# Attention and a spectral gate on one core: three batches' DMA transposes moved from SyncE's queue to ScalarE's, with a new hand-tuned order

## The chip, the cores and the metric

The kernel runs on one core of one Trainium2 chip. The metric is the device time of one execution in microseconds, as the median of several runs; smaller is better. The profile is that of a single execution on the same core, so its span (382.9 us) is a little under the median of the runs.

## What is computed

Eight batches of an attention with 12 heads (448 rows, 64 columns a head) feed a gated spectral filter:

```python
scores = q @ k.T / 8;  m = max(scores);  e = exp(scores - m)
x = (e / (sum(e) + exp(-m))) @ v          # per head, then heads side by side: 448 x 768
x1, x2, x3 = split(x @ w_proj, 3)          # 768 -> 3 * 768
x2 = irfft(rfft(x2) * rfft(filter))        # a circular convolution over the 448 rows
out = (x1 * x2 * x3) @ w_out               # 448 x 768, float32
```

All matmuls are in bf16. The softmax runs without the maximum: numerator and denominator are multiplied by exp(m), so the denominator is sum(e) + 1.

## The kernel before, in words

**The work.** Heads go in pairs, six pairs to a batch, 48 in all. For one pair TensorE forms the scores with the keys on partitions (L773, and L775 for the keys left over, which both heads share), ScalarE takes their exponentials into bf16 (L780, L786), TensorE multiplies them with v (L798 for the shared keys, L806 for the rest), and VectorE divides by the sum (L819 to L821) and writes the tile `xb`, rows on partitions. The dense part wants x with its columns on partitions, in the tile `xT`. There are two ways from `xb` to `xT` (`attention`, end): four TensorE transposes into PSUM (L901) and a copy back (L908 on ScalarE, L910 on VectorE), or one DMA transpose of two or three pairs (`x_dma`, L892). Which of them is taken is set by `XALL`: a batch in it turns all six pairs by DMA; another batch from the third on turns five by DMA and the last on TensorE; the first two turn all on TensorE.

**The dense part of a batch** is in `dense(b)`: VectorE folds `xT` (L950 to L958), TensorE forms x2 from the folded columns (L981, or L1011 and a DMA transpose back, L1028, in the last four batches), ScalarE and VectorE carry the spectrum (L1049, L1057, L1063, L1069), TensorE forms the gates x1 and x3 (`gate`, L1095), ScalarE copies x1 out (L1107), VectorE multiplies by x3 (L1110); TensorE goes back from the spectrum (L1134, L1143), VectorE unfolds and multiplies into `yT` and `yR` (L1152 to L1178), and TensorE multiplies with w_out (L1207). ScalarE copies that to `osb` (L1219), and SyncE stores it (L1226; L1229 for the 64 rows left over, which two batches share). The dense part of a batch runs between the attention of later batches.

**Loads and other transposes.** From the third batch on q, k and v come as DMA loads (q on GpSimd's queue, L536; k and v on SyncE's, L585, then cast to bf16 on GpSimd, L590 and L602), and q and k are turned by DMA transposes on SyncE's queue (L542, four to a batch; L547, two blocks of 12 x 128 columns to a batch from the fourth on). All DMA transposes of the kernel before stand in SyncE's queue.

**What sets the order.** Nothing is scheduled by loops. Every piece of work is a task with an engine, a cost, a wanted time and the tokens that it needs and makes (`add`). `Plan.run` plays the tasks through at the written costs, lets each engine take the first of its tasks, in the order of wanted times, whose needs are met, and hands out PSUM banks. The tasks of each engine are emitted in that order, and each engine then works its own list strictly from the top. The wanted times come from the tables at the head of the kernel (`ATT`, `SLOT`, `DENSE`, `PACE`, `FOLD`, `LEAD`, ...), `late` is an extra landing time that the planner books for a transfer. The waits between engines are put in by the framework when the program is built. In the gaps that the planner sees in the first 36 us it puts small matmuls on a tile of zeros (L1332).

**The end.** In the last batch the rows 256 to 383 (block 2) come last. `O_last` writes them in three pieces, of 384, 192 and 192 columns, copies the last piece on VectorE and stores each by itself.

Of the kernel before, what the change touches and what calls it, by code (L numbers as in the profile page):

```python
# [19 lines left out]
D = H * DH  # L20
SP = 112
NST = S // SP
NDT = D // 128
NHP = H // 2
SCALE = 1.0 / float(np.sqrt(DH))
DCH = 384
# [15 lines left out]
class Plan:  # L42
# [26 lines left out]
    def add(self, eng, cost, want, emit, need=(), make=(), take=(), give=(), dma=0.0, run=256, n=1, after=0.0, begun=(), late=0.0):  # L69
        self.tasks.append((want, len(self.tasks), eng, cost, emit, need, make, take, give, dma, after, run, n, begun, late))  # L70
# [186 lines left out]
def kernel(  # L257
# [11 lines left out]
    nc = tc.nc  # L269
# [1 line left out]
    MAGIC = 12582912.0  # L271
    NSTAGED = 2
    SPIN = 38
    EARLY1 = 2.19
    ATT = [0.75, 24.41, 87.21, 101.61, 150.77, 186.69, 235.26, 286.49]
    SLOT = [2.52, 8.01, 4.27, 4.82, 6.44, 0.30, 6.71, 5.19]
    DENSE = [46.81, 84.00, 123.83, 169.80, 218.58, 253.46, 313.76, 296.92]
    PACE = [2.16, 2.30, 2.04, 2.28, 1.15, 2.55, 0.60, 1.33]
    FOLD = [-0.20, 0.45, -42.13, -39.60, 2.51, 0.15, -6.85, 0.77]
    BPS = 1.67  # L280
    RE1 = 22.20
    WT = 1.31
    FT = 21.96
    HALVED = (2,)
    AHEAD = [0, 0, 33.95, 43.62, 34, 34, 34, 34]
    LEAD = [-14.87, 8.62, 5.03, 10.66]
    LOADS = ((1, 0), (1, 1), ("F", None), (0, None), (2, None), ("O", None))
    LOAD = [22.29, 18.40, 18.46, 37.27, 38.16, 45.94]
    STEP = 2.26
    BYCOL = (4, 5, 6, 7)  # L290
    GLAST = 40.00
    XALL = (3, 4, 5, 6, 7)
    FOLD0 = (52.22, 39.65, 43.44)

    const = ctx.enter_context(tc.tile_pool(name="const", bufs=1))
    wts = ctx.enter_context(tc.tile_pool(name="wts", bufs=1))
# [16 lines left out]
    wout_bf = wts.tile([128, NDT, D], BF16, name="wout_bf")  # L313
# [8 lines left out]
    kT = [const.tile([128, NHP, 4, 128], BF16, name=f"kT{i}") for i in range(2)]  # L322
# [14 lines left out]
    nf = nat.bitcast(F32)  # L337
# [13 lines left out]
    add = plan.add  # L351
# [4 lines left out]
    def bank(hy):  # L356
        i = plan.banks[hy][0]
        return psum[:, 512 * i : 512 * i + 512]
# [167 lines left out]
    def loaded(b):  # L526
# [3 lines left out]
        parts = 2 if b in HALVED else 1  # L530
        size = NHP // parts
        few = 1 if b == NSTAGED else 3
# [20 lines left out]
        n = 0  # L553
# [21 lines left out]
        for hp in range(NHP):  # L575
            g = i0 + hp
            for n, (name, x) in enumerate((("k", k), ("v", v))):
                slot = 2 * (g - NHP * NSTAGED) + n
                at = (KNAT + NST * D) // 2 + 384 * (slot % 5)
                src = nf[:, at : at + 384]  # L580
                old = slot - 5
                room = [("c" + "kv"[old % 2], NHP * NSTAGED + old // 2)] if old >= 0 else [
                    ("c" + w, i) for w in "kqv" for i in range(NHP * NSTAGED - 2, NHP * NSTAGED)]
                add("SP", 0.52, tau(g) - LEAD[0] + 0.1 * n,
                    lambda x=x, hp=hp, src=src: nc.sync.dma_start(src.rearrange("p (u c) -> p u c", u=2), rows(x, b, hp)),  # L585
                    need=room, make=[("s" + name, g)], dma=0.7, run=768)
                sv = src.rearrange("p (u j d) -> p u j d", u=2, j=3)
                if name == "k":
                    add("POOL", 0.6, tau(g) - LEAD[1],
                        lambda hp=hp, sv=sv: nc.gpsimd.tensor_copy(  # L590
                            kn[:, hp, 1:4].rearrange("p j (u d) -> p u j d", u=2), sv
                        ),
                        need=[("sk", g)] + (["zero kn"] if b == NSTAGED else [("kT", g - NHP)]), make=[("ck", g)])
                    if hp % few == 0:
                        gs = range(g, g + few)
                        add("SP", 1.3, tau(g) - LEAD[2], lambda hp=hp: k_turn(hp), need=[("ck", i) for i in gs] + [("crk", b), last],
                            make=[("kT", i) for i in gs], dma=0.6 * few, late=0.7)
                else:

                    def cast(hp=hp, sv=sv):  # L600
                        for u in range(2):
                            nc.gpsimd.tensor_copy(vn[b % 2][:, hp, 4 * u : 4 * u + 3, 0:DH], sv[:, u])  # L602

                    add("POOL", 0.72, tau(g) - LEAD[3], cast, need=[("sv", g), ("V", g - 2 * NHP, 1)], make=[("cv", g), ("v", g)])
# [104 lines left out]
    W = {}  # L709
# [51 lines left out]
    def attention(i):  # L761
# [127 lines left out]
        def x_dma():  # L889
            x, xb = xT(), W["xb", b]  # L890
            gs = slice(0 if hp < 3 else 3, hp + 1)
            nc.sync.dma_start(  # L892
                x[:, gs, :].rearrange("p g (t n) -> p (g t) n", t=NST),
                xb[:, gs].rearrange("p g t c -> p (g t c)"),
                transpose=True,
            )
# [18 lines left out]
        if b in XALL or b > 1 and hp < NHP - 1:  # L915
            if hp in (2, NHP - 1 if b in XALL else NHP - 2):
                ps = range(0, 3) if hp == 2 else range(3, hp + 1)
                add("SP", 1.3, w, x_dma, need=[("xb", NHP * b + h) for h in ps] + old,
                    make=[m for h in ps for m in (("X", NHP * b + h), ("xT", b, h))], dma=0.5 * len(ps), late=1.2)
        else:  # L920
            add("PE", 0.23, w, x_pe, need=[("xb", i)], make=[("X", i)], take=[("hy", ("X", i))])
            add("ACT" if on_act else "DVE", 0.43 if on_act else 0.33, w - 1.0, x_back, need=[("X", i)] + old, make=[("xT", b, hp)], give=[("hy", ("X", i))])


    def dense(b):

        L = {}
        at = [0.0, 0]

        def span(cost):  # L930

            w = DENSE[b] + at[0] * PACE[b]
            at[0] += cost
            return w
# [9 lines left out]
        def hold(key):  # L944
            return ("hy", key)
# [88 lines left out]
        def PT(dt):  # L1034
            hy = hold(("PT", b, dt))
            w = span(1.15)
            add("PE", 1.15, w, lambda: columns(dt, hy), need=[("xf", b, pg) for pg in range(4)] + [("w", 1, ch) for ch in range(2)],
                make=[("PT", b, dt)], take=[hy], give=[("xf", b)])
            add(("ACT", "DVE")[dt % 2], (0.43, 0.55)[dt % 2], w, lambda: columns_back(dt), need=[("PT", b, dt)],
                make=[("x2T", b, dt // 3)], give=[hy])  # L1040
            if dt % 3 == 2:
                ch = dt // 3
                add("SP", 1.3, w, lambda: rows_back(ch), need=[("x2T", b, ch)], make=[("x2", b, pg, ch) for pg in range(4)],
                    take=[("x2", b)], dma=1.5, late=1.2)

        def spectrum(pg, ch, hy):
            K = BLK_K[pg]
# [199 lines left out]
            if ch == 1:  # L1247
                add("SP", 0.6, w, lambda: store(st), need=[("os", b, st)], make=[("store", b, st)], give=[os_], dma=1.4, run=3072)

        def O_last(st):  # L1250
            rs = slice(st * 128, (st + 1) * 128)
            parts = ((0, DCH, "ACT"), (DCH, DCH // 2, "ACT"), (DCH + DCH // 2, DCH // 2, "DVE"))
            for n, (at, size, by) in enumerate(parts):
                hy = hold(("O", b, st, n))
                w = span(0.97 * size / DCH)
                c = slice(at, at + size)

                def product(hy=hy, c=c, size=size, n=n):
                    L["O", st, n] = bank(hy)
                    for dt in range(NDT):  # L1260
                        nc.tensor.matmul(
                            L["O", st, n][:, 0:size], W["yT", b][:, dt, rs], wout_bf[:, dt, c], start=(dt == 0), stop=(dt == NDT - 1)
                        )

                def back(size=size, c=c, n=n, by=by):
                    (nc.scalar.copy if by == "ACT" else nc.vector.tensor_copy)(nf[:, c], L["O", st, n][:, 0:size])

                def store_part(c=c, n=n):
                    (nc.scalar if n == 1 else nc.sync).dma_start(out[b, rs, c], nf[:, c])

                add("PE", 0.98 * size / DCH, w, product, need=[("y", b, 0), "wout"], make=[("O", b, st, n)], take=[hy],
                    give=[("yT", b)])
                add(by, (0.38, 0.25, 0.28)[n], w, back, need=[("O", b, st, n)], make=[("os", b, st, n)], give=[hy])
                add("ACT" if n == 1 else "SP", 0.6, w, store_part, need=[("os", b, st, n)], make=[("store", b, st, n)],
                    dma=1.4 * size / D, run=1536)

        if b and b + 1 < n_batches:
            G(0, 0), G(0, 1)
        if b in BYCOL and b + 1 == n_batches:
# [21 lines left out]
        for dt in range(NDT):  # L1301
            I(dt), G(2 + (dt + 1) // 2, (dt + 1) % 2)
        G(5, 1)
        for st in range(3) if b % 2 == 0 and b + 1 < n_batches else (0, 1, 3, 2) if b + 1 == n_batches else range(4):
            if (b, st) == (n_batches - 1, 2):
                O_last(st)
                continue
            for ch in range(2):
                O(st, ch)


    E = mybir.EngineType
# [103 lines left out]
```

## Time and profile before

| | before |
|---|---|
| median of 3 runs | 385.62 us (385.33 to 387.34) |
| span of the profiled execution | 382.9 us |
| TensorE busy | 366.5 us (96%), 3678 matmuls |
| ScalarE busy | 261.2 us (68%) |
| VectorE busy | 258.0 us (67%) |
| GpSimd busy | 112.5 us (29%) |
| DMA moved | 62.53 MB, mean 163 GB/s |

Engines are written PE (TensorE matmuls), PEld (its weight loads), DVE (VectorE), ACT (ScalarE), POOL (GpSimd) and SP (SyncE); SPq and ACTq are the DMA issues of an engine. In a list of waits, "PE psum L1095 <- DMA xT<-xb" says that a matmul of line 1095 sat idle until a transfer from `xb` to `xT` had landed. In a timeline a row has start, length, engine, line, operation and tiles, and in brackets the idle time ahead of it with what ended it. A chain of waits is followed back from the last instruction, at each step to what released it.

### The profile page before, as it was taken

Reading aid. Unit: us, or ns where it says so; the run is one execution under the profiler, and the core shown is the slowest. Engines: PE = TensorE matmul, PEld = TensorE weight load, DVE = VectorE, ACT = ScalarE, POOL = GpSimd, SP = SyncE. Lnnn points to the kernel's source line nnn. Section 1 sums busy time; section 2 is a strip of 40 time slices with the busy share of each in tenths; the row PEclk is TensorE's granted clock in tenths of the full one; section 3 lists DMA queues with packets and bytes.
Section 4 is the critical chain, followed back from the end, with each engine's and each line's share of the span. In section 5 each row is a group of like instructions: output and inputs, shape, how many; then the busy total and the mean of one; then the engine's idle time right before and its main releaser. Section 6 shows DMA issues by size and latency. Waiting matters only on the chain.

```text
span 382.9 us, 9526 instructions
## 1 busy us (share of the span) xinstructions
PE 366.5 (96%) x3678; PEld 225.7 (59%) x3678; DVE 258.0 (67%) x671; ACT 261.2 (68%) x456; POOL 112.5 (29%) x232
## 2 busy tenths in 40 slices
PE   8879999999999999959999999999999999999995
PEld 7557765566655675635675555555555655655553
DVE  6587589945789549747367964783469936982880
ACT  5867875756877878845688846675788758633633
POOL 6695465032464434704345350000000000000000
PEclk9998999999999999998999999999999999999999
DMA  8999999999999999999899998942341034046205
GB/s 214 276 258 249 227 204 210 117 138 247 203 201 220 138 294 235 176 150 276 232 220 159 206 235 140 174 128 84 84 85 34 9 96 113 6 80 137 111 0 166
DMA packets 149965, 62.53 MB, mean 163 GB/s; under 512 B 114525, under 2 KB 146464, under 8 KB 149920
## 3 DMA queue, kind: packets, MB, share of 16 engines
q1 hardware_dynamic: 112352, 52.05, 63.0%
q0 software_dynamic: 37184, 9.54, 25.4%
q8 instruction: 29, 0.48, 0.5%
q10 hardware_dynamic: 384, 0.33, 0.3%
q14 instruction: 16, 0.13, 0.1%
HBM read 43.86 MB, written 11.01 MB: 143 GB/s over the span
## 4 chain that ended last, share of the span: by engine, by line
PE 81%; DVE 8%; DMA 4%; issue 3%; SPq 1%; ACT 1%; POOL 1%; DVEq 0%; POOLq 0%
PE psum L1095 25%; PE psum L1207 13%; PE psum L806 9%; PE psum L981 8%; PE psum L773 7%; PE psum L1011 7%; PE psum L1049 3%; DMA xT<-xb 2%; PE psum L1134 2%; PE psum L775 2%; DMA nat<-in_q_dram 2%; PE psum L798 1%; DVE xb L821 1%; DVE xf L958 1%; PE psum L901 1%
## 5 line engine op out<-in xcount | busy, mean ns | idle before, releaser
L780 ACT ACTIVATE e<-psum 128x896 bf16<-128x896 f32 x144 | 125.6, 925 | 23.1 <-PE psum L773 22.0
L1095 PE MATMUL psum<-xT,wproj_bf 128*128 128x448 bf16 x576 | 121.9, 354 | 5.1 <-DMA xT<-xb 4.2
L1095 PEld LDWEIGHTS <-wproj_bf 128*128 128x128 bf16 x576 | 54.6, 98 | 51.5 <-issue 8.3
L1207 PE MATMUL psum<-wout_bf,yT 128*128 128x384 bf16 x276 | 50.6, 326 | 0.0
L1107 ACT CAST x<-psum 128x448 bf16<-128x448 f32 x48 | 25.8, 537 | 29.8 <-PE psum L1095 27.1
L806 PE MATMUL psum<-vn,e 128*128 128x65 bf16 x1152 | 45.3, 195 | 0.0
L1219 ACT COPY osb<-psum 128x384 f32<-128x384 f32 x54 | 25.2, 483 | 23.9 <-PE psum L1207 23.4
L773 PE MATMUL psum<-qT,kT 64*128 64x448 bf16 x288 | 41.1, 356 | 0.0
L806 PEld LDWEIGHTS <-e 128*128 128x128 bf16 x1152 | 39.5, 98 | 2.6
L1063 DVE TENSOR_TENSOR t<-xs,hrs 113x768 bf16<-113x768 bf16 (+1 forms) x64 | 33.5, 563 | 8.6 <-ACT xs L1057 8.4
L602 POOL CAST vn<-nat 128x192 bf16<-128x192 f32 x72 | 28.2, 418 | 34.8 <-DMA nat<-in_v_dram 25.3
L819 DVE TENSOR_SCALAR rec<-psum 128x8 f32<-128x8 f32 x48 | 7.8, 163 | 44.7 <-PE psum L806 33.8
L1207 PEld LDWEIGHTS <-yT 128*128 128x128 bf16 x276 | 26.2, 97 | 18.2 <-issue 1.1
L536 POOL DMA_DIRECT2D nat<-in_q_dram x28 | 24.8, 888 | 36.2 <-DMA qT<-nat 26.8
L1110 DVE TENSOR_TENSOR g<-x,psum 128x448 bf16<-128x448 bf16 x48 | 29.5, 616 | 8.3 <-PE psum L1095 6.3
L981 PE MATMUL psum<-wproj_bf,xf 128*113 128x384 bf16 x192 | 35.0, 327 | 0.0
L821 DVE TENSOR_TENSOR xb<-psum,rec 128x512 bf16<-128x512 f32 x48 | 33.2, 691 | 1.7
L1011 PE MATMUL psum<-xf,wproj_bf 128*128 128x452 bf16 x144 | 30.4, 356 | 0.0
L1057 ACT CAST xs<-psum 113x384 bf16<-113x384 f32 (+1 forms) x64 | 27.5, 500 | 3.5 <-PE psum L1049 3.3
L786 ACT ACTIVATE er<-psum 128x448 bf16<-128x448 f32 x48 | 26.9, 560 | 3.2 <-PE psum L775 2.8
L981 PEld LDWEIGHTS <-xf 128*113 128x113 bf16 x192 | 24.8, 132 | 6.8 <-issue 0.7
L1143 ACT CAST cr<-psum 128x452 bf16<-128x452 f32 x48 | 24.7, 557 | 5.9 <-PE psum L1134 5.9
(117 smaller groups left out, 461.7 us busy)
## 6 DMA issues: line engine op xcount, KB each, us to landing
nat<-in_k_dram SPq DMA_DIRECT2D x48, 192.0 KB, 5.5
nat<-in_v_dram SPq DMA_DIRECT2D x48, 192.0 KB, 5.5
out_dram<-osb SPq DMA_DIRECT2D x23, 384.0 KB, 3.2
nat<-in_q_dram POOLq DMA_DIRECT2D x20, 168.0 KB, 7.6
nat<-in_q_dram SPq DMA_DIRECT2D x11, 224.0 KB, 6.0
wproj_bf<-in_moe_w_proj_dram POOLq DMA_DIRECT2D x2, 1152.0 KB, 16.9
rests<-in_k_dram SPq DMA_DIRECT2D x8, 192.0 KB, 6.1
rests<-in_v_dram SPq DMA_DIRECT2D x8, 192.0 KB, 6.9
```

The costliest lines, as they stand in the source:

```text
L602: nc.gpsimd.tensor_copy(vn[b % 2][:, hp, 4 * u : 4 * u + 3, 0:DH], sv[:, u])
L773: nc.tensor.matmul(sc[:, u, 0:S], kT[b % 2][c, hp, t, :], qT[b % 2][c, hp, :])
L780: nc.scalar.activation(e[:, 0 : 2 * S].rearrange("p (u n) -> p u n", u=2), pair(("sc", ("S", i, t)))[:, :, 0:S], AF.Exp, scale=SCALE,)
L806: nc.tensor.matmul(out_bank(u)[:, n, :], P["e"][1 + t][:, u * S + n * 128 : u * S + n * 128 + 128], vn[b % 2][:, hp, 4 * u + t, :], start= ...
L821: nc.vector.tensor_tensor(W["xb", b][:, hp].rearrange("p n (u d) -> p u n d", u=2), op[:, :, :, 0:DH], rec[:].unsqueeze(3).to_broadcast([1 ...
L981: nc.tensor.matmul(pps[:FQ, :DCH], W["xf", b][:, pg, kt, 0:FQ], wproj_bf[:, kt, D + ch * DCH : D + (ch + 1) * DCH], start=(kt == 0), stop= ...
L1011: nc.tensor.matmul(pps[:, 0 : 4 * FQ], wproj_bf[:, kt, D + dt * 128 : D + (dt + 1) * 128], W["xf", b][:, :, kt, 0:FQ], start=(kt == 0), st ...
L1057: nc.scalar.copy(L["xs", par, ch][:K, pg % 2, :], L["Z", pg, ch][:K, :DCH])
L1063: nc.vector.tensor_tensor(t[:K], L["xs", par, ch][:K], h, op=ALU.mult)
L1095: nc.tensor.matmul(p[:, :S], wproj_bf[:, kt, 2 * part * D + dt * 128 : 2 * part * D + (dt + 1) * 128], xT()[:, kt, 0:S], start=(kt == 0), ...
L1110: nc.vector.tensor_tensor(g[:, dt, :], L["x1", dt], p[:, :S], op=ALU.mult)
L1207: nc.tensor.matmul(ops[:n, :DCH], y[:, dt, 0:n], wout_bf[:, dt, ch * DCH : (ch + 1) * DCH], start=(dt == 0), stop=(dt == NDT - 1),)
```

## The change

The DMA transposes of x of the third, fourth and fifth batch (`b < 5`: six instructions) are issued from ScalarE's queue, so that they need not stand in line behind the loads and the transposes of q and k in SyncE's queue. The fourth and fifth batch leave `XALL`: they turn their last pair on TensorE, and their second DMA transpose carries two pairs, not three. `O_last` goes, and the last batch writes its outputs in a new order, with the last row block in two whole pieces of 384 columns and one store. The planner books more landing time for the transposes of k (1.5 for 0.7) and of x2 (2.5 for 1.2), and all tables of wanted times have new values.

```diff
-    ATT = [0.75, 24.41, 87.21, 101.61, 150.77, 186.69, 235.26, 286.49]
-    SLOT = [2.52, 8.01, 4.27, 4.82, 6.44, 0.30, 6.71, 5.19]
-    DENSE = [46.81, 84.00, 123.83, 169.80, 218.58, 253.46, 313.76, 296.92]
-    PACE = [2.16, 2.30, 2.04, 2.28, 1.15, 2.55, 0.60, 1.33]
+    ATT = [0.79, 17.21, 90.53, 105.41, 147.12, 188.78, 237.77, 285.73]
+    SLOT = [2.38, 8.68, 4.01, 3.23, 6.89, 0.31, 4.90, 5.05]
+    DENSE = [43.97, 82.34, 125.97, 170.34, 220.10, 253.73, 311.48, 304.06]
+    PACE = [1.76, 2.32, 1.55, 2.33, 1.19, 2.38, 0.76, 1.20]
...
-    AHEAD = [0, 0, 33.95, 43.62, 34, 34, 34, 34]
-    LEAD = [-14.87, 8.62, 5.03, 10.66]
+    AHEAD = [0, 0, 48.31, 45.28, 34, 34, 34, 34]
+    LEAD = [-24.87, 14.95, 5.88, 4.42]
...
-    XALL = (3, 4, 5, 6, 7)
+    XALL = (5, 6, 7)
...
                         add("SP", 1.3, tau(g) - LEAD[2], lambda hp=hp: k_turn(hp), need=[("ck", i) for i in gs] + [("crk", b), last],
-                            make=[("kT", i) for i in gs], dma=0.6 * few, late=0.7)
+                            make=[("kT", i) for i in gs], dma=0.6 * few, late=1.5)
...
-            nc.sync.dma_start(
+            (nc.scalar if b < 5 else nc.sync).dma_start(
                 x[:, gs, :].rearrange("p g (t n) -> p (g t) n", t=NST),
                 xb[:, gs].rearrange("p g t c -> p (g t c)"),
                 transpose=True,
...
-                add("SP", 1.3, w, x_dma, need=[("xb", NHP * b + h) for h in ps] + old,
+                add("ACT" if b < 5 else "SP", 1.3, w, x_dma, need=[("xb", NHP * b + h) for h in ps] + old,
...
-                    take=[("x2", b)], dma=1.5, late=1.2)
+                    take=[("x2", b)], dma=1.5, late=2.5)
...
-        def O_last(st):
...
-        for st in range(3) if b % 2 == 0 and b + 1 < n_batches else (0, 1, 3, 2) if b + 1 == n_batches else range(4):
-            if (b, st) == (n_batches - 1, 2):
-                O_last(st)
-                continue
-            for ch in range(2):
+        if b + 1 == n_batches:
+            for st, ch in ((0, 0), (0, 1), (1, 0), (3, 0), (3, 1), (1, 1), (2, 0), (2, 1)):
                 O(st, ch)
+        else:
+            for st in range(3 + b % 2):
+                for ch in range(2):
+                    O(st, ch)
```

More of the change, by code (lines that the diff above doesn't have):

```diff
@@ L273 @@
     SPIN = 38
-    EARLY1 = 2.19
-    ATT = [0.75, 24.41, 87.21, 101.61, 150.77, 186.69, 235.26, 286.49]
-    SLOT = [2.52, 8.01, 4.27, 4.82, 6.44, 0.30, 6.71, 5.19]
-    DENSE = [46.81, 84.00, 123.83, 169.80, 218.58, 253.46, 313.76, 296.92]
-    PACE = [2.16, 2.30, 2.04, 2.28, 1.15, 2.55, 0.60, 1.33]
-    FOLD = [-0.20, 0.45, -42.13, -39.60, 2.51, 0.15, -6.85, 0.77]
-    BPS = 1.67
-    RE1 = 22.20
+    EARLY1 = 5.03
+    ATT = [0.79, 17.21, 90.53, 105.41, 147.12, 188.78, 237.77, 285.73]
+    SLOT = [2.38, 8.68, 4.01, 3.23, 6.89, 0.31, 4.90, 5.05]
+    DENSE = [43.97, 82.34, 125.97, 170.34, 220.10, 253.73, 311.48, 304.06]
+    PACE = [1.76, 2.32, 1.55, 2.33, 1.19, 2.38, 0.76, 1.20]
+    FOLD = [-0.20, 0.39, -46.27, -39.52, 1.71, 0.19, -8.61, 0.59]
+    BPS = 1.80
+    RE1 = 13.75
     WT = 1.31
-    FT = 21.96
+    FT = 20.85
     HALVED = (2,)
-    AHEAD = [0, 0, 33.95, 43.62, 34, 34, 34, 34]
-    LEAD = [-14.87, 8.62, 5.03, 10.66]
+    AHEAD = [0, 0, 48.31, 45.28, 34, 34, 34, 34]
+    LEAD = [-24.87, 14.95, 5.88, 4.42]
     LOADS = ((1, 0), (1, 1), ("F", None), (0, None), (2, None), ("O", None))
-    LOAD = [22.29, 18.40, 18.46, 37.27, 38.16, 45.94]
-    STEP = 2.26
+    LOAD = [18.82, 18.41, 10.28, 37.96, 41.97, 46.86]
+    STEP = 1.79
     BYCOL = (4, 5, 6, 7)
     GLAST = 40.00
-    XALL = (3, 4, 5, 6, 7)
-    FOLD0 = (52.22, 39.65, 43.44)
+    XALL = (5, 6, 7)
+    FOLD0 = (63.46, 45.82, 34.40)
     const = ctx.enter_context(tc.tile_pool(name="const", bufs=1))
@@ L1248, in O @@
                 add("SP", 0.6, w, lambda: store(st), need=[("os", b, st)], make=[("store", b, st)], give=[os_], dma=1.4, run=3072)
-        def O_last(st):
[L1251 to L1275, printed above, removed]
         if b and b + 1 < n_batches:
```

## The prediction

> **What bounds the kernel now.** I read the busy shares first.
>
> ```profile
> PE 366.5 (96%) x3678; PEld 225.7 (59%) x3678; DVE 258.0 (67%) x671; ACT 261.2 (68%) x456; POOL 112.5 (29%) x232
> ```
>
> TensorE leaves 16.4 us of the span, so the time is TensorE's work plus its gaps, and a change can win little but can lose much: each us that TensorE stands still is a us of the result. Next, the list of waits of TensorE alone (us in total, times, longest):
>
> ```profile
> PE psum L1095 <- DMA xT<-xb: 4.2, 1, 4.2
> PE psum L901 <- DVE xb L821: 3.4, 2, 2.4
> PE psum L474 <- POOL q L431: 1.1, 1, 1.1
> ```
>
> One gap is large: a gate matmul that waits for the DMA transpose of x. The rest is at the start and the end. The timelines of TensorE and of SyncE's queue around it (start, length):
>
> ```profile
> 166.40 1.86 PE L1095 MATMUL psum<-xT,wproj_bf 128*128 128x448 bf16 x9
> 172.50 0.73 PE L1095 MATMUL psum<-xT,wproj_bf 128*128 128x448 bf16 x3 [4.23 <-DMA xT<-xb]
> 173.93 1.50 PE L806 MATMUL psum<-vn,e 128*128 128x65 bf16 x24
> 175.25 2.12 PE L1095 MATMUL psum<-xT,wproj_bf 128*128 128x448 bf16 x6
> ```
>
> ```profile
> 155.41 4.20 SPq L542 DMA_TRANSPOSE qT<-nat  x3
> 161.02 1.60 SPq L542 DMA_TRANSPOSE qT<-nat  x1
> 163.06 4.16 SPq L892 DMA_TRANSPOSE xT<-xb  x1
> ```
>
> x of the fourth batch's last three pairs was issued from 163.06 and landed 9.39 us later, behind four transposes of q. The gap has a tail: 24 matmuls of L806 then took 1.50 us (0.93 in the groups before), six of L1095 2.12 (1.30). That is 1.4 us of half speed, so this stall costs 4.2 + 1.4 = 5.6 us. It is what the change goes after.
>
> How long a set of transposes takes on SyncE's queue is shown best by the seventh batch's, four of q and one block of k back to back. First the timeline of the queue, then the k block in the DMA issues of that stretch and in those of 125 to 127 us (last number: us to landing), then all of xT:
>
> ```profile
> 194.88 5.55 SPq L542 DMA_TRANSPOSE qT<-nat  x4
> 200.52 1.47 SPq L547 DMA_TRANSPOSE kT<-nat  x1
> ```
>
> ```profile
> kT<-nat SPq DMA_TRANSPOSE x1, 5.3
> ```
>
> ```profile
> kT<-nat SPq DMA_TRANSPOSE x1, 7.2
> ```
>
> ```profile
> DMA to landing us min/median/max: 3.2/3.8/10.1
> ```
>
> From the first issue to the landing of the k block that is 200.52 + 5.3 - 194.88 = 10.9 us.
>
> [...] issues are 1.2 to 1.5 us, landings 3.2 to 10.1. [...] L892 stood in single waits of up to 3.6 us there. [...]
>
> **The change, part by part.** In the built order of the changed kernel the six transposes of x stand in ScalarE's list with waits in front of them: each waits for the completion of every transpose that SyncE's list has before it, not for its data alone. While ScalarE stands there, everything queued behind it stands too: exponentials (L780), copies of x1 (L1107), of outputs (L1219), of the spectrum (L1057). TensorE waits for these. Two of the six (first parts of the third and fifth batch) wait for k blocks that stand some 9 us and 16 us of TensorE work earlier; I cost these at nothing but the issue, which VectorE's and TensorE's queued work hides. For the other four I count from the first of the waited-for issues to the first TensorE instruction that cannot go on.
>
> *Fourth batch, second part.* In front of it stand four q transposes and one k block (the sixth batch's), as in the set of 194.88: the last lands 10.9 us after the first issue. The first is released by a scores matmul. From there TensorE has, at the start-to-start spacings of these groups in the timelines, 8 of L798 (0.2), 24 of L806 (0.86), one L775 (0.2), 4 of L1134 (0.2), 12 of L1095 (2.27) and 12 of L1207 (1.95): 5.7 us. The next L1207 needs the last pair of yT, and that hangs on ScalarE: after the landing come the issue (1.3), the x1 copy (0.53), the gate product (0.61), the product into yT (0.56) and hand-overs (0.2), 3.2 us. Stall: 10.9 + 3.2 - 5.7 = 8.4 us. With the k block at 3.7 us, the page's median for the x2 transposes of the same size, it is 6.8.
>
> *Fifth batch, second part.* The same five in front, the same TensorE work behind: 8.4 us again.
>
> *Third batch, second part.* In front: q, k block, q. The k block issues 1.2 us after the first and took 7.2 us to land in that stretch: 8.4. TensorE has 8 of L798, L775, 24 of L806, 12 of L1207, 4 of L773 (0.4), 8 of L798, 24 of L806, L775: 4.9 us; the next L1207 needs a PSUM bank that the first exponential behind the transpose empties: issue 1.3, L780 0.93, 0.1. Stall 8.4 + 2.3 - 4.9 = 5.8; with 5.3 us to land, 3.9. I take 5.
>
> *Fourth batch, first part.* In front: the second k block of the fifth batch, which needs casts on GpSimd of k loads. If it issues at its place, 5.5 us of TensorE work ahead of the blocked matmul (L1049, waiting for a copy of L1057), it lands 5.5 us later (the median of all k blocks), and with 1.3 for the issue, 0.5 for the copy and 0.1 the stall is 5.5 + 1.9 - 5.5 = 1.9 us. But in the trace of before the loads run late here: the first k block of the fifth batch issued at 142.09, some 7.5 us after the TensorE work beside it in the order, and the second at 152.34. With 10.25 us between the two, the 6.0 us that the second took to land, and 10 us of TensorE work from the first to the blocked matmul, the stall is 10.25 + 6.0 + 1.9 - 10 = 8.2, more if the first is late too. I take 6, ends 1.9 and 10.
>
> Holds together: 8.4 + 8.4 + 5 + 6 = 27.8 us (ends 19 and 33).
>
> *Removed:* the stall of 5.6 us. x of the fourth batch's second part now has 10 us of TensorE work between its place and its gate, plus the hold.
>
> *Half clock:* each hold leaves TensorE idle for longer than the 4.23 us that brought 1.4 us of half speed. I count two: 2.8 (ends 0 and 6).
>
> *Last pair on TensorE:* 8 transposes more at 0.057 us spacing, 0.46 us, and two L910 copies of 0.38 on VectorE, which has a third of its time free. +0.5.
>
> *The end:* the last row block goes in two wholes. Its matmuls take 2 x 0.98 for 2.13 (-0.2); its last copy 0.48 for 0.36 (+0.1), its store 384 KB for 96, 3.2 us to land for 2.8 (+0.4). +0.3.
>
> *All other tables and the `late` values* move tasks about. Fill matmuls are 90 for 89, so the planner sees the same start; otherwise TensorE does the same work. I cost them at 0, ends -2 and +2.
>
> Sum: 27.8 - 5.6 + 2.8 + 0.5 + 0.3 = +25.8; 385.6 + 25.8 = 411.
>
> **The rivals.** *Only the two five-transposes sets hold; in the others the waits are nearly over, or all holds are about half as long.* For: later stalls give the late loads time to catch up. Against: the set's 10.9 us has issues in it that can't overlap. 385.6 + 16.8 - 5.6 + 2.8 + 0.8 = 400; with halved holds 385.6 + 13.9 - 5.6 + 0.8 = 395. *ScalarE's wait is free:* SyncE issues early enough that the transposes have landed when ScalarE comes; then only the 5.6 us are won: 385.6 - 5.6 + 0.8 = 381. For: ScalarE is idle 32% of the time. Against: in the built order the last SyncE transpose stands only 0.1 to 0.6 us of TensorE work ahead of three of the six, and no landing in the trace is under 2.3 us. *A wash,* a gain as large as the holds: small, since it needs holds of just 5 to 7 us.
>
> **How the numbers follow.** Four holds at 411: 0.60. The middle cases, 392 to 402: 0.26. Free wait, 381: 0.10. A wash: 0.04. The range leaves out the last two and the top of the first (33 us of holds with full half clock gives about 422): 392 to 421. Faster by over 0.5%: 0.10; within: 0.04; slower: 0.86.
>
> **What would show it.** Right: in the waits of the changed kernel ScalarE stands before L892 for 5 to 9 us, with a transfer to qT or kT as releaser, and TensorE's list shows gaps of 4 us and more with L1057, L1107 or the chain to yT behind them; the gap on xT is gone. Wrong: TensorE idle stays near 16 us; or ScalarE's gaps are there and TensorE works through them, because the first matmul that needs ScalarE comes later than I counted; or SyncE's sets land in much under 10 us.

## The result, and the profile after

The changed kernel takes 440.5 us (median; 439.7 to 441.9) against 386.1 us: 1.141 times the time before, 95% interval 1.137 to 1.146. The forecast was 411 us (392 to 421). The direction and the mechanism came as written; the increase, 54.4 us, was about twice the 25.8 us that the sum gave, and the time lies outside the range.

The busy shares of the changed kernel (span 439.2 us; the columns are those shown of before):

```profile
PE 377.6 (86%) x3681; PEld 227.4 (52%) x3681; DVE 254.4 (58%) x672; ACT 262.3 (60%) x456; POOL 111.8 (25%) x232
```

The span grew by 56.3 us, in two parts: TensorE's idle time went from 16.4 to 439.2 - 377.6 = 61.6 us (+45.2), and its busy time from 366.5 to 377.6 us (+11.1) for three matmuls more. ScalarE's busy time is nearly unchanged (262.3 us for 261.2), so it is not more work that made it late.

The list of waits of TensorE, changed kernel:

```profile
PE psum L1207 <- DVE yT L1178: 24.6, 2, 13.2
PE psum L1095 <- ACT cr L1143: 10.3, 1, 10.3
PE psum L1049 <- ACT xs L1057: 8.3, 1, 8.3
PE psum L1207 <- ACT e L780: 5.4, 1, 5.4
```

The gap on xT is gone, and five new gaps of together 48.6 us stand in its place. Below, "hold" is a stretch in which ScalarE stands in front of a transfer of x, and "stall" the idle time of TensorE that comes of it. Three of the gaps name ScalarE as releaser. The two on yT do not, and there the chain of waits has to be followed back. The second of them, from the chain of the changed kernel between 245 and 267 us (start, length, what):

```profile
253.05 9.39 DMA kT<-nat
...
262.62 1.25 ACTq L892
...
263.96 0.54 ACT x L1107
...
264.52 0.63 DVE g L1110
...
265.18 0.57 DVE yT L1178
...
265.80 1.46 PE psum L1207 x4
```

This is the chain of the prediction link by link: the landing of a k block, the issue of x on ScalarE, the copy of x1 that stood behind it, gate product, product into yT, matmul. From the landing at 262.44 to the issue at 262.62 are 0.2 us; the matmuls of the copied x1 had ended at 250.6, and the copy ran behind the issue, at 263.96, after 14.57 us in which ScalarE did no work but the issue. The wait goes the other way too. SyncE's queue in the same stretch, and a line of the list of what SyncE waited for:

```profile
247.01 5.99 SPq L542 DMA_TRANSPOSE qT<-nat  x4
253.05 13.95 SPq L547 DMA_TRANSPOSE kT<-nat  x2
```

```profile
SPq L547 <- DMA xT<-xb: 9.5, 1, 9.5
```

Of the two k blocks the second was issued at 265.73, only once x, issued at 262.62 with 3.0 us to land, was there; TensorE's list of waits names no transfer to kT.

The five holds against the prediction, with the landing of the last transfer that ScalarE waited for:

| x of | forecast | stall | last landing waited for |
|---|---|---|---|
| third batch, first part | 0 | 10.3 | k block, issued 111.56, 6.0 us |
| third batch, second part | 5 | 5.4 | q, issued 136.12, 4.7 us |
| fourth batch, first part | 6 | 8.3 | k block, issued 166.75, 4.6 us |
| fourth batch, second part | 8.4 | 11.4 | k block, issued 196.09, 8.3 us |
| fifth batch, first part | 0 | 0 | k block, landed 11.6 us before x was issued |
| fifth batch, second part | 8.4 | 13.2 | k block, issued 253.05, 9.4 us |

### The profile page after: what moved, and what is told of

Same layout as the page of the kernel before. It is cut to its first block, busy times and chain, and to the rows that moved or that the text cites. A ratio compares the mean times of both kernels' runs of the same rounds, so it can differ in the third digit from the quotient of the medians.

```text
span 439.2 us, 9544 instructions
## 1 busy us (share of the span) xinstructions
PE 377.6 (86%) x3681; PEld 227.4 (52%) x3681; DVE 254.4 (58%) x672; ACT 262.3 (60%) x456; POOL 111.8 (25%) x232
## 4 chain that ended last, share of the span: by engine, by line
PE 57%; DMA 16%; DVE 11%; SPq 5%; ACT 4%; issue 3%; POOL 2%; ACTq 1%; DVEq 0%; POOLq 0%
PE psum L1095 18%; PE psum L1207 10%; PE psum L1011 6%; PE psum L806 6%; PE psum L773 5%; DMA kT<-nat 5%; DMA nat<-in_v_dram 5%; PE psum L981 3%; DMA qT<-nat 3%; DVE t L1063 3%; SPq L542 3%; PE psum L775 1%; DVE g L1110 1%; DVE yh L1069 1%; ACTq L892 1%
## 5 line engine op out<-in xcount | busy, mean ns | idle before, releaser
L1095 PE MATMUL psum<-xT,wproj_bf 128*128 128x448 bf16 x576 | 123.4, 360 | 10.6 <-ACT cr L1143 10.3
L1095 PEld LDWEIGHTS <-wproj_bf 128*128 128x128 bf16 x576 | 55.7, 99 | 68.7 <-issue 26.0
L1207 PE MATMUL psum<-wout_bf,yT 128*128 128x384 bf16 x288 | 56.0, 346 | 30.0 <-DVE yT L1178 24.6
L1107 ACT CAST x<-psum 128x448 bf16<-128x448 f32 x48 | 25.8, 537 | 59.8 <-PE psum L1095 32.0
L1207 PEld LDWEIGHTS <-yT 128*128 128x128 bf16 x288 | 28.8, 102 | 52.2 <-DVE yT L1178 25.8
L602 POOL CAST vn<-nat 128x192 bf16<-128x192 f32 x72 | 26.6, 388 | 91.6 <-PE psum L806 56.9
L1063 DVE TENSOR_TENSOR t<-xs,hrs 113x768 bf16<-113x768 bf16 (+1 forms) x64 | 34.4, 574 | 23.1 <-ACT xs L1057 23.1
L1219 ACT COPY osb<-psum 128x384 f32<-128x384 f32 x56 | 26.1, 484 | 30.2 <-PE psum L1207 27.5
L1057 ACT CAST xs<-psum 113x384 bf16<-113x384 f32 (+1 forms) x64 | 27.3, 502 | 13.0 <-DMA nat<-in_v_dram 10.1
L1143 ACT CAST cr<-psum 128x452 bf16<-128x452 f32 x48 | 23.9, 557 | 15.4 <-DMA nat<-in_v_dram 12.0
```

Of the source, the lines that this page charges most:

```text
L1057: nc.scalar.copy(L["xs", par, ch][:K, pg % 2, :], L["Z", pg, ch][:K, :DCH])
L1063: nc.vector.tensor_tensor(t[:K], L["xs", par, ch][:K], h, op=ALU.mult)
L1095: nc.tensor.matmul(p[:, :S], wproj_bf[:, kt, 2 * part * D + dt * 128 : 2 * part * D + (dt + 1) * 128], xT()[:, kt, 0:S], start=(kt == 0), ...
L1207: nc.tensor.matmul(ops[:n, :DCH], y[:, dt, 0:n], wout_bf[:, dt, ch * DCH : (ch + 1) * DCH], start=(dt == 0), stop=(dt == NDT - 1),)
```

## The experiments

### Is it the queue?

Two kernels take the change apart. The first is the changed kernel with the queue of before; the second is the kernel before with only the new queue.

```diff
 # the changed kernel, queue of before
-            (nc.scalar if b < 5 else nc.sync).dma_start(
+            nc.sync.dma_start(
```

> The changed kernel with its six transposes of x issued from SyncE's queue again; the planned order, all new tables, the last pair on TensorE and the new end stay. Theory (ScalarE's waits for SyncE's transposes cost the time): all five stalls of 5.4 to 13.2 us go, with their half-speed tails, so 440.5 - 48.6 - 7 = 385, within 5; TensorE's idle time falls from 62 to under 25 us. Rival (the new tables put work into a bad order, and the stalls only show where): it stays above 420. What is left over 386 is the cost of the tables and the late transposes; under 386, their gain.

Measured: 390.3 us, 1.010 of before (1.006 to 1.015). All five stalls are gone; TensorE is idle for 389.3 - 368.5 = 20.8 us. Its longest waits:

```profile
PE psum L1134 <- DVE g L1110: 3.8, 3, 2.9
PE psum L901 <- DVE xb L821: 3.5, 3, 2.2
```

The time lies 0.3 us beyond the theory's bound; what is left over 386 us is looked at below.

```diff
 # the kernel before, new queue
-            nc.sync.dma_start(
+            (nc.scalar if b < 5 else nc.sync).dma_start(
...
-                add("SP", 1.3, w, x_dma, need=[("xb", NHP * b + h) for h in ps] + old,
+                add("ACT" if b < 5 else "SP", 1.3, w, x_dma, need=[("xb", NHP * b + h) for h in ps] + old,
```

> The kernel before with only the queue changed: its six transposes of x of the third to fifth batch (fourth and fifth batch with three pairs in the second part) are issued from ScalarE and planned there; all tables, XALL and the end are those of before. In its order the same waits stand in ScalarE's list, five of the six for a k block or four q and a k block. Theory: 430 to 445, with TensorE stalls of 5 to 13 us behind copies and exponentials of ScalarE. Rival (the tables and not the queue): about 386, within 4.

Measured: 433.2 us, 1.123 of before (1.117 to 1.130). The list of waits of TensorE:

```profile
PE psum L1207 <- ACT e L780: 16.5, 2, 8.6
PE psum L1095 <- ACT e L780: 9.6, 1, 9.6
PE psum L1095 <- ACT cr L1143: 8.9, 1, 8.9
PE psum L1049 <- ACT xs L1057: 5.2, 1, 5.2
```

Again five holds, of 40.2 us together, all behind work of ScalarE. With the old tables the queue alone costs 46.5 us, with the new ones 440.5 - 390.3 = 50.2 us. The rival that blamed the tables for the whole is out.

### Is it the wait, or the issuing?

The six transfers stay in ScalarE's queue, at the same places, as plain copies of the same bytes, which leave x of these batches unturned.

```diff
-            (nc.scalar if b < 5 else nc.sync).dma_start(
+            if b < 5:
+                nc.scalar.dma_start(
+                    x[:, gs, :].rearrange("p g n -> p (g n)"), xb[:, gs].rearrange("p g t c -> p (g t c)")
+                )
+                return
+            nc.sync.dma_start(
```

> The changed kernel with its six transfers from ScalarE as plain copies of the same bytes (x of the third to fifth batch is left unturned, so those batches' output is not the reference's). Plain copies wait for their data alone, not for SyncE's transposes; issue time on ScalarE and all orders stay. Theory (the waits alone cost): no stall longer than 5 us, time 380 to 390. Rival (issuing a DMA from ScalarE costs ScalarE the time, or the transfers themselves collide): over 410.

Measured: 400.6 us, 1.041 of before (1.034 to 1.048): between theory and rival. Three of the five stalls are gone, two are not (lines after L892 stand five further down here, L1148 is L1143 and L1062 is L1057):

```profile
PE psum L1054 <- ACT xs L1062: 7.4, 1, 7.4
PE psum L1100 <- ACT cr L1148: 4.5, 1, 4.5
```

The chain of waits ahead of the second shows what ScalarE's queue waited for:

```profile
112.38 3.80 DMA rests<-in_k_dram
...
116.26 0.59 ACTq L893
...
116.89 0.55 ACT cr L1148
...
117.48 2.40 PE psum L1100 x6
```

By the chain it stood for the landing of a load of k's remaining rows (L566) that the copy does not read; VectorE had written the last of x at 110.84, 5.4 us earlier. Ahead of the 7.4 us stall it is a load of v (L585), issued at 158.27 and landed at 161.81, with the copy at 161.89 and the last of x written at 153.07. In the built order of the changed kernel, too, each of these transfers has such a wait beside those for the transposes: for one earlier load in SyncE's list. I had read those lists for the transposes only. The next kernel moves just these two copies to SyncE.

```diff
-                nc.scalar.dma_start(
+                (nc.sync if hp == 2 and b < 4 else nc.scalar).dma_start(
```

> As the kernel with plain copies (x of the third to fifth batch left unturned, those batches' output is not the reference's), but two of the six copies, the first parts of the third and fourth batch, are issued from SyncE. With plain copies the chain of waits ended these two at the landing of loads of SyncE's list (L566, L585), which they do not read. Theory (a ScalarE transfer also waits for one such earlier SyncE transfer, and where SyncE is late that is a hold of its own): the stalls of 4.5 and 7.4 us go, 400.6 - 11.9 = 389, within 3. Rival (SyncE's lateness would hold TensorE there in any case, by k or by x): 396 or more.

Measured: 387.7 us, 1.004 of before (1.002 to 1.007). No trace of this kernel is read, so that the two stalls went is taken from the time alone: the 12.9 us won lie near their 11.9 us. So issuing a plain copy from ScalarE costs next to nothing of itself; what costs is standing, there, for something of SyncE's list, and that need not be a transpose. Two things stay open. A plain copy occupies ScalarE's list for 0.47 to 0.59 us, a transpose in the changed kernel for 1.25 to 2.24 us, and what this difference costs was not measured alone. And why the program puts in the wait for that one load was not tested.

### The hold that I had costed at nothing

The first part of the third batch alone goes back to SyncE.

```diff
-            (nc.scalar if b < 5 else nc.sync).dma_start(
+            (nc.scalar if b < 5 and (b, hp) != (2, 2) else nc.sync).dma_start(
```

> The changed kernel with one of the six, the first part of the third batch, issued from SyncE. This is the one whose hold I had costed at nothing and which shows 10.3 us. Theory A (each hold is a cost of its own): the 10.3 us stall and its half-speed tail of about 2 us go, 440.5 - 12.3 = 428, within 3. Theory B (SyncE and GpSimd are behind there, and the stall only let them catch up): the next holds at 143 and 174 us grow by as much, and the time stays at 435 to 441.

Measured: 428.9 us, 1.111 of before (1.106 to 1.115), 11.6 us less than the changed kernel: Theory A. The list of waits keeps the other four:

```profile
PE psum L1207 <- DVE yT L1178: 21.2, 2, 12.6
PE psum L1049 <- ACT xs L1057: 8.6, 1, 8.6
PE psum L1207 <- ACT e L780: 5.8, 1, 5.8
```

The stall is a cost of its own; the next two grew by 0.4 us each, from 5.4 and 8.3. That the saving comes so near the forecast is in part luck: the last two shrank, from 11.4 and 13.2 to 8.6 and 12.6, and in front of the first of these the k block landed in 5.5 us for 8.3.

That leaves why the k block of the first hold landed so late. The timelines of SyncE's queue and then of ScalarE, changed kernel:

```profile
107.40 0.42 SPq L585 DMA_DIRECT2D nat<-in_k_dram  x1
110.52 0.37 SPq L566 DMA_DIRECT2D rests<-in_k_dram  x1
...
111.56 2.37 SPq L547 DMA_TRANSPOSE kT<-nat  x1
```

```profile
107.05 0.55 ACT L786 ACTIVATE er<-psum 128x448 bf16<-128x448 f32 x1
117.64 1.89 ACTq L892 DMA_TRANSPOSE xT<-xb  x1
119.57 0.97 ACT L1143 CAST cr<-psum 128x452 bf16<-128x452 f32 x2 [11.97 <-DMA nat<-in_v_dram]
```

Ahead of the k block in SyncE's queue is a load of k's remaining rows (L566). It stood until 110.52 for a buffer that GpSimd's casts empty (L570, from 109.41), and ahead of these casts GpSimd stood idle for 3.12 us in front of its next load of q (108.48), until a transpose of q, issued at 99.81, had landed at 107.92 and freed the tile. So the k block went out at 111.56, while the TensorE work beside it in the order ran at 98.7, and landed at 117.54. ScalarE had come to x at 107.6. (The bracket in the last row names another load as releaser; the landing that ends together with the wait is the k block's.)

### Why the last two holds are longer than 8.4 us

In the sets ahead of them the q transposes went out as in the prediction (5.6 to 6.0 us for four); the k block took 8.3 and 9.4 us to land instead of 5.3. The DMA view of the changed kernel from 253 to 263 us shows what ran beside it:

```profile
q0 software_dynamic: 5440, 0.69, 126.3%
q1 hardware_dynamic: 2267, 0.56, 47.5%
...
nat<-in_q_dram POOLq DMA_DIRECT2D x3, 168.0 KB, 7.0
...
kT<-nat SPq DMA_TRANSPOSE x1, 9.4
```

A row of a queue gives packets, MB, and the time of all its packets as a share of the stretch on the 16 DMA engines. The packets of GpSimd's q loads (q0), released by the q transposes just ahead, took 126%, those of the other queue 47%; shares over 100% mean that packets were in flight at the same time. To test this, these loads also wait for the k block of the batch before. (By the edit that is its first k block, the one that ScalarE waits for; the expectation says "second".)

```diff
-                room = [("c" + w, i0 - 2) for w in "kqv"] if b == NSTAGED else [("qturn", b - 1, st)]
+                room = [("c" + w, i0 - 2) for w in "kqv"] if b == NSTAGED else [("qturn", b - 1, st)] + ([("kT", i0 - NHP)] if b > 4 else [])
```

> The changed kernel, where the q loads on GpSimd's queue for the sixth to eighth batch also wait for the second k block of the batch before, so that they no longer run while the k block lands that ScalarE's wait ends with. Theory (the k block takes 8.3 and 9.4 us to land, not 5.3, because these q loads run beside it): it lands in 4.5 to 6 us, the last two stalls shrink from 11.4 and 13.2 to some 8 and 9, and the time is 432 to 436. Rival (the k block is slow for other reasons, such as the q transposes ahead of it): the two stalls stay within 1 us of 11.4 and 13.2 and the time within 2 of 440.5.

Measured: 429.1 us, 1.110 of before (1.106 to 1.115), 11.4 us less than the changed kernel. The DMA view of the same step, now at 247 to 253 us, and the waits on yT:

```profile
q1 hardware_dynamic: 2570, 0.63, 54.6%
...
kT<-nat SPq DMA_TRANSPOSE x1, 3.7
```

```profile
PE psum L1207 <- DVE yT L1178: 14.4, 2, 7.5
```

Without loads beside it the k block lands in 3.7 us (in the fourth batch's set too), and the two stalls are 6.9 and 7.5 us. That is the lower end of the prediction, 6.8 us with the k block at 3.7. The time fell to 3 us below the range that I expected. In the other sets the landing follows the same way: with 0.12 MB of q loads moved beside it the k block landed in 5.3 us (kernel before, the set of 194.88), with 0.36 MB in 5.5 (the kernel with one part back on SyncE), with 0.47 and 0.69 MB in 8.3 and 9.4 (changed kernel; in all but the last, loads of k or v were issued meanwhile as well). A longer landing also lets more of q pass, so this row alone would prove nothing; the kernel with the later loads does. In what way the loads hold the k block back is not shown.

### The other parts of the change

The end and the last pair on TensorE, each alone in the kernel before, and the two together:

```diff
 # the end alone (shortened)
-        for st in range(3) if b % 2 == 0 and b + 1 < n_batches else (0, 1, 3, 2) if b + 1 == n_batches else range(4):
...
+        if b + 1 == n_batches:
+            for st, ch in ((0, 0), (0, 1), (1, 0), (3, 0), (3, 1), (1, 1), (2, 0), (2, 1)):
...
 # the last pair alone
-    XALL = (3, 4, 5, 6, 7)
+    XALL = (5, 6, 7)
```

> The kernel before with the end of the changed one alone: the last batch's outputs in the new order, the last row block in two whole pieces and one store. My step said +0.3 us (store 384 KB instead of 96, copy on ScalarE), so 386 within 1 of the kernel before. Rival (the pieces are worth more, because the store's landing is the end of the span): +1 to +2.

Measured: 386.1 us, 1.000 of before (0.998 to 1.003). No difference is seen; +0.3 us is too small to be told from none here.

> The kernel before with the fourth and fifth batch out of XALL: their last pair turns on TensorE, the second DMA transpose carries two pairs and is asked for one pair earlier; queue, tables and end as before. My step said +0.5 us for the turning itself. Theory (the 5.6 us stall on xT stays, since it is the queue's): 384 to 388. Rival (going one pair earlier is enough to bring x in time without ScalarE's queue): 380 to 382.

Measured: 382.4 us, 0.989 of before (0.986 to 0.992): 0.4 us above the rival's range and well under the theory's, so the rival, and a version that beats both kernels. The waits on xT are gone without another queue. The DMA views of this kernel from 158 to 161 us and of the kernel before from 163 to 164 us show the transfer concerned, x of the fourth batch's second part:

```profile
q1 hardware_dynamic: 2389, 0.59, 95.8%
...
xT<-xb SPq DMA_TRANSPOSE x1, 3.1
```

```profile
q0 software_dynamic: 435, 0.06, 95.7%
q1 hardware_dynamic: 49, 0.14, 72.3%
...
xT<-xb SPq DMA_TRANSPOSE x1, 9.4
```

Asked for one pair earlier, x goes out at 158.87 instead of 163.06, before any packet of the q loads (q0) moves instead of beside them, and lands in 3.1 us for 9.4. Here the transfer is also one pair smaller, so this pair of views alone does not separate the two causes; the k blocks above, of one size, do.

> The kernel before with the fourth and fifth batch out of XALL and the end of the changed kernel, so all of the change but the queue, the two landing times of the planner and the tables. By the single runs: 382.4 + (386.14 - 386.31) = 382 within 1. With 390.3 for all but the queue, the tables would then cost 8. Rival (the end costs when TensorE is not late): 384 or more.

Measured: 382.7 us, 0.992 of before (0.990 to 0.995), as the two parts gave. The changed kernel with SyncE's queue has all of this and the tables and landing times besides (and x still planned as ScalarE's), at 1.010. So these together cost 0.018 of 386 us, about 7 us, where I had put 0 with ends of 2. Which of the three does it, the tables, the landing times or the planning of x on an engine that does not issue it, was not tested.

Two more kernels look for gains of the same kind: the sixth batch out of XALL too, and the fourth batch's second part (which stood behind the stall of before) turned on TensorE altogether.

```diff
 # the sixth too
-    XALL = (3, 4, 5, 6, 7)
+    XALL = (6, 7)
 # the fourth's second part on TensorE
-        if b in XALL or b > 1 and hp < NHP - 1:
+        if (b in XALL or b > 1 and hp < NHP - 1) and not (b == 3 and hp > 2):
```

> The kernel before with the sixth batch out of XALL too (only the seventh and eighth turn all pairs by DMA). Theory (the gain of taking the fourth and fifth out, 3.9 us, was the one stall on xT; the sixth has no such stall): 382 to 384. Rival (a general gain from handing the last pair to TensorE): another 1 us or more, under 381.5.

Measured: 383.4 us, 0.995 of before (0.992 to 0.997). The sixth batch adds nothing, so the gain is not a general one of handing the last pair to TensorE.

> The kernel before with the second part of the fourth batch (pairs four to six), the one behind the 5.6 us stall, turned on TensorE, with no DMA transpose; all else as before. Expected: the stall goes (-5.6), 12 transposes of 0.057 us and three copies come in (+0.7, copies off the path), so 381, within 2. Rival (the copies out of PSUM fall on ScalarE and VectorE just where the gates need them, or another wait is next in line): 385 to 388.

Measured: 385.0 us, 0.995 of before (0.992 to 0.997). The stall is gone from the profile, but the gain is 2 us, not 5: a miss, and at the rival's edge. The profile of the last-pair kernel shows where such a gain goes. Its idle time on TensorE, 380.5 - 363.9 = 16.6 us, looks no smaller than before, and its busy time fell from 366.5 to 363.9 us. But most of the busy time "won" lies in the first 40 us, long before the batches that were changed. The stretch from 0 to 40 us, first of the kernel before, then of the last-pair kernel (start and end, length, then busy time and instructions of PE, PEld, DVE, ACT, POOL, then the granted clock):

```profile
0.00:40.00 40.00, 34.75 (x480) 26.25 (x480) 27.92 (x77) 29.48 (x46) 27.81 (x70) 0.96 1.09 248
```

```profile
0.00:40.00 40.00, 32.59 (x478) 24.49 (x480) 28.32 (x77) 29.23 (x46) 26.49 (x68) 1.00 1.09 245
```

For nearly the same matmuls single executions differ there by 2.2 us of busy time; the kernel with the last pair and the new end even has 35.36. From 40 us on busy time is 331.8 and 331.3 us and idle time 11.1 and 9.2 us. So 1.9 of the 4.2 us of idle are won, and small waits took the rest, among them two of the last-pair kernel that the kernel before does not have:

```profile
PE psum L1049 <- DVE x L996: 1.5, 2, 1.1
...
PE psum L1207 <- DVE xb L821: 0.8, 1, 0.8
```

## Why the prediction was wrong in size

*The wait.* Right, though not the whole of it. The trace, and the two kernels that change the queue alone, show that ScalarE's stand before L892 makes the time. Why the built program has these waits is not shown by any run. The prediction named only transposes as what ScalarE waits for; with plain copies it still stood for two loads, behind stalls of 4.5 and 7.4 us. The three rivals fall: halved holds and a wash by the size, the free wait by the five holds in the trace.

*"Two of the six ... wait for k blocks that stand some 9 us and 16 us of TensorE work earlier; I cost these at nothing but the issue."* This step failed for the first of them: 10.3 us of stall, 11.6 us in the run without it. I measured the distance in the order, in TensorE's time, but the k block goes out when SyncE comes to it, 13 us after its neighbours on TensorE. For the fourth batch's first part I did ask when SyncE would be there, and came near (6, measured 8.3). For the fifth batch the step held.

*The two that came near.* Part of that is luck. For the fourth batch's first part the two k blocks went out 7.4 us apart for the 10.25 that I took, and the second landed in 4.6 us for 6.0; with the 3.0 us from there to the matmul the same sum makes 7.4 + 4.6 + 3.0 - 10 = 5.0, so the rest is the first one's lateness. For the third batch's second part (5, measured 5.4) I let a k block land last, 8.4 us after the first issue; in the trace it was the q transpose behind it, after 7.7 us.

*"8.4 us" for the sets of five.* The chain was right; one term was mis-sized: the k block's landing, 5.3 us from a set that had only 0.12 MB of the next batch's q loads beside it, measured 8.3 and 9.4. That is 3.0 and 4.1 of the 3.0 and 4.8 us that the stalls were longer. The prediction did not ask what else would be moved while it landed.

*"Half clock: I count two: 2.8."* Mis-sized, in number and in length. The prediction says itself that each hold is longer than the 4.23 us that brought half speed, and gives no reason for counting two. The granted clock of TensorE, in parts of full speed, was 0.51 from 174 to 177 us of the kernel before, behind its 4.23 us; in the changed kernel it was 0.50 behind each of the five stalls (over 120.1 to 122.5, 143.3 to 146, 174.3 to 178, 207.8 to 211 and 265.8 to 270 us). One stretch of 10 us with such a gap, first of the kernel before, then of the changed kernel (start and end, length, busy time and instructions of PE, PEld, DVE, ACT, POOL, then the granted clock):

```profile
170.00:180.00 10.00, 7.35 (x61) 4.03 (x61) 7.15 (x17) 4.32 (x6) 5.15 (x10) 0.83 1.35 243
```

```profile
260.00:270.00 10.00, 4.20 (x14) 1.78 (x16) 1.32 (x3) 2.12 (x5) 0.00 (x0) 0.50 1.02 135
```

The last stall as the timeline of TensorE shows it, with the same twelve matmuls ahead of the gap:

```profile
250.44 2.11 PE L1207 MATMUL psum<-wout_bf,yT 128*128 128x384 bf16 x12
265.80 4.02 PE L1207 MATMUL psum<-wout_bf,yT 128*128 128x384 bf16 x12 [13.24 <-DVE yT L1178]
269.75 0.93 PE L773 MATMUL psum<-qT,kT 64*128 64x448 bf16 x4
```

Twelve matmuls in 4.02 for 2.11 us and the next four in 0.93 for 0.55 are 2.3 us. Counted alike, the stretch after the 5.4 us stall has 2.5, so between these two the loss does not grow with the gap. In all, TensorE's busy time grew by 11.1 us where the prediction's terms make 2.8 + 0.5 - 1.4 = 1.9; as single executions differ by some 2 us of busy time at the start, this is a rough figure. The mean granted clock of the two profiled executions is 0.937 for 0.990.

*The sum.* Over the forecast of 25.8 us come 10.3 (the hold costed at nothing), 7.8 (the two sets of five), 2.7 (the other two holds) and 9.2 (clock): 30.0 us, and 55.8 with it, for a measured 56.3 between the two spans (54.4 between the medians). The 7 us of the tables, the landing times and the planning of x, put at 0 in the prediction, don't show in it as a term: TensorE's idle time outside the five holds is 61.6 - 48.6 = 13.0 us, against 20.8 with SyncE's queue. That the holds hide small waits is a likely reading, but only argued.

*The removed stall.* Its 4.2 us of idle went, as forecast, but taking the last pair out does that without the new queue. And 5.6 us was too much: the two kernels that remove it gain 4 and 2 us by their ratios. It was the figure of one execution; in the trace of the kernel with only the new end, which keeps this queue, the same wait is 2.8 us. "Behind four transposes of q" was half of the reading: the q loads moved beside x as well.

*"Issues are 1.2 to 1.5 us."* That is the usual case; the prediction's own timeline has one of 4.16. On ScalarE the six took 1.25 to 2.24 us; in the two sets of five it was the 1.3 of the sum.

*The end.* +0.3 forecast, nothing measurable: not contradicted.

## What to carry to other kernels

Before a transfer is moved to a compute engine's queue, list every completion that the built program makes it wait for, the loads too, and ask for each when the other queue really gets there and what else is moved while it lands (q loads made 9.4 us of 3.7 here); what stood behind the transfer in ScalarE's list stood with it, 14.57 us at the longest. Distances in the planned order say nothing where one queue is known to run late (13 us in the first hold). A transfer that comes too late in its queue is mended more cheaply by asking for it earlier or making it smaller, which won 1.1% here, than by issuing it from ScalarE, which cost 12%.

## What I had not expected of the hardware

A DMA transpose of one k block (12 x 128 columns) landed in 3.7 us with nothing of GpSimd's queue beside it and in 8.3 and 9.4 us with q loads there: 0.47 and 0.69 MB of q, moved while it landed, more than double it. And, a trait of the built program and not shown to be one of the chip: a plain copy from ScalarE's queue stood 5.5 and 8.7 us until a load had landed that it does not read, which gave TensorE stalls of 4.5 and 7.4 us.
